# Attention transposes in two 64-row halves, with shared PSUM banks, split pools and a new written order

## The chip, the cores and the metric

One core of one Trainium2 chip. The metric is the device time of one execution in microseconds (us), the median of the runs. Engines: TensorE (PE in the rows, PEld for its weight loads), VectorE (DVE), ScalarE (ACT), GpSimd (POOL) and SyncE (SP, which here only issues DMAs).

## The reference

Three parts in a row, all in float32:

- Attention: q, k, v of shape (2, 8, 576, 64): batch 2, 8 heads, 576 positions, 64 numbers a head. q and k get a rotary embedding, then `softmax(q k^T / 8) v` for each head. The softmax divides by the sum plus 1e-9.
- A feed-forward layer on the 1152 x 512 result: `h = x @ w_in` (512 x 2048), `g = h * sigmoid(1.702 h)`, `g @ w_out`.
- A top-1 mixture of 8 experts (512 to 1024 to 512 with a ReLU) with a capacity for each expert; each token's row is scaled by the softmax probability of its expert.

## The kernel before, in words

Class `Attention` does the first part, class `Weights` loads the feed-forward weights and turns their 64-bit numbers into float32 (a "cut": three VectorE instructions, L530 to L532), class `Experts` does the rest. The change lies in `Attention` and in the constants at the top of the file.

Attention goes over 8 head pairs p (4 a batch). A pair's 576 queries are split in two halves a, each of two 128-row tiles t and 32 left over; with two heads h that makes 8 score tiles of 128 queries x 576 keys, and tile 4 holds the left-over queries of both heads. For each tile i:

- `scores` (L346, tile 4 at L337): matmuls of 64 rows (one head) against 288 keys, into a PSUM tile `s` of two banks. The two heads' matmuls stand in turn, on the upper and the lower 64 rows. TensorE does a float32 matmul in two instructions, a transpose in one.
- `least` (L358, VectorE): scales a score tile out of PSUM into `pp` and finds its minimum.
- `exps` (L370, ScalarE): exponential and row sum.
- `turn` (L389, TensorE): four 128x128 transposes of the tile into a bank `t`; `turned` (L276 on ScalarE, L277 on VectorE, both in the helper `copy`) copies the bank to `pt`.
- Columns 512 to 575 of two heads are transposed together: `rest` (L407, L409), placed in `ptr`. The reciprocals of the sums are spread over 64 columns (`spread`) and transposed (`sums`, L430, L432), placed in `tb`. `placed` copies them, with two small picks for a = 0.
- `weighted` (L451): for each half a, 10 products of v and `pt` or `ptr`, each of 128 rows x 64 columns x 288, two heads side by side, summed in PSUM bank `o`.
- `divided` (L454, VectorE): times the reciprocals; `halved` (hi at L276/L277, lo at L464): result into `xt` as a float32r number and its remainder.

PSUM of attention is 8 banks: `s` two tiles of 2, `t` three of 1, `o` 1. `next` hands out the `s` and the `t` tiles in turn. All SBUF tiles of attention come from one pool "at", all PSUM tiles from one pool "at_ps"; their room goes to `Experts` behind it.

The rotary embedding (`rope`, L321, L323) of pair 0 is on VectorE, in pieces (`START`), and of later pairs on GpSimd, two pairs ahead.

The order is written out by hand. `plan` gives every step of every pair a time: 9 units per pair, plus the tile number, plus an offset in `ORDER`; the steps are sorted by it. `pin` chains the instructions of each engine in that order, so each engine does them in this order, waiting at the head of its queue where an operand isn't ready. `ENGINES` says which engine copies what. The steps "spare" are the loads and cuts of the first 4 of 16 slices of the feed-forward weights, 8 cuts; `ORDER["spare"]` has the plan time of the first cut and the step between cuts.

Behind attention, for each weight slice, ScalarE and VectorE write a hi and a lo part (L617, L618) into a ring of 4 (`hl`, 32 KB of each partition), the first thing allocated in the room that attention had. TensorE then multiplies (`hidden`, L631, and L657) 480, 384 and 288 tokens in three passes over the slices. The first 480 tokens are all of batch 0.

Tile allocation and waits come from a scheduling layer: an instruction that writes to room which an older pool had waits for the readers of that pool.

Of the kernel before, what the change touches and what calls it, by code (L numbers as in the profile page):

```python
# [9 lines left out]
F32 = mybir.dt.float32  # L10
# [32 lines left out]
TC = {"schedule_with_timeline_sim": True}  # L43
CUT = 352
START = (
    (-7.97, 0, 0, CUT, "vector"),
    (-5.96, 1, 0, P, "vector"),
    (-5.82, 0, CUT, WIDTH, "vector"),
    (-5.66, 1, P, 2 * P, "vector"),
    (-8.85, 1, 2 * P, WIDTH, "gpsimd"),  # L50
)
# [32 lines left out]
CUTS = 0, 5, 9, 12  # L84
WIDE = max(b - a for a, b in zip(CUTS, CUTS[1:])) * TT
ORDER = {
    "scores": (-3.87, 3.28, -2.97, -0.67, -3.82, -3.5, 2.97, -3.53, -0.45),
    "least": (-2.82, -2.97, -2.63, -2.15, -2.74, -2.49, -3.28, -2.19, -2.98),
    "exps": (-2.07, -2.94, -1.17, -0.62, -2.47, -1.81, -2.57, -1.96, -2.28),
    "turn": (-0.4, -0.09, -0.77, -0.34, -0.01, -0.18, -0.84, -1.22, 0.22),  # L90
    "turned": (-0.09, 1.98, 0.73, 0.74, 0.29, 0.5, 0.71, 0.42, 0.25),
    "twice": 4.24,
    "rest": (4.75, 9.15),
    "rest_placed": (5.5, 9.76),
    "inverse": (2.9, 6.22),
    "spread": (3.76, 7.85),
    "sums": (5.5, 9.37),
    "sums_placed": (6.72, 9.92),
    "weighted": ((5.94, 5.98, 6.1, 7.03, 7.44), (9.47, 9.62, 10.57, 11.02, 11.65)),
    "divided": (8.36, 12.05),  # L100
    "halved": ((8.99, 11.5), (13.17, 15.47)),
    "rope": (-10.84, -10.42, -8.78, -9.18, -8.94, -7.53),
    "load": (-17.9, -17.6),
    "load_v": -5.18,
    "spare": (59.64, 5.42),
}


# [126 lines left out]
class Attention:  # L235


    def __init__(self, ctx, tc, qk, v, cst, xt):
        self.tc, self.nc = tc, tc.nc
        self.src = qk, v  # L240
        self.xt, self.cst = xt, cst
        self.ident = cst["ident"]
        pool = ctx.enter_context(tc.tile_pool(name="at", bufs=1))
        ps = ctx.enter_context(tc.tile_pool(name="at_ps", bufs=1, space=PSUM))
        new = self.new = lambda name, *shape: pool.tile([P, *shape], F32, name=name)
        some = lambda n, name, *shape: [new(f"{name}{i}", *shape) for i in range(n)]
        self.turns = new("turns", 2, WIDTH + 64)
        self.qk = some(3, "qk", 4, WIDTH)
        self.vr = some(2, "vr", 10, D)
        self.pp = some(4, "pp", 2, S)  # L250
        self.prem = new("prem", WIDTH)
        self.pt = new("pt", 4, 2, 2, HALF)
        self.ptr = new("ptr", 2, HALF)
        self.tb = new("tb", 2, HALF)
        self.x = some(2, "x", HALF)
        self.nm, self.sum, self.r = (some(2, name, 9) for name in ("nm", "sum", "r"))
        self.rr = some(2, "rr", 2, 2, 64)
        self.s = [ps.tile([P, 2, 512], F32, name=f"s{i}") for i in range(2)]
        self.t = [ps.tile([P, 512], F32, name=f"t{i}") for i in range(3)]
        self.o = ps.tile([P, 512], F32, name="o")[:, 0:HALF]  # L260
        self.made = {"s": 0, "t": 0}
        self.open = {}
        self.last = {}

    def next(self, of, key):
        mine = getattr(self, of)
        self.open[key] = x = mine[self.made[of] % len(mine)]
        self.made[of] += 1
        return x

    def engine(self, part):
        return getattr(self.nc, ENGINES[part])
# [56 lines left out]
    def scores(self, p, i):  # L329
# [61 lines left out]
    def turned(self, p, i):  # L391
        t = self.open.pop(("turn", p, i))
        if i == 4:
            x = t.rearrange("p (k r) -> p k r", r=32)
            out = self.pt.rearrange("p k h a c -> p (k h a) c")[:, :, 256:288]
        else:
            a, tt, h = TILES[i]
            x = t.rearrange("p (k c) -> p k c", k=4)
            out = self.pt[:, :, h, a, tt * P:(tt + 1) * P]
        self.copy(self.engine(f"t{i}"), out, x)  # L400

    def rest(self, p, a):

        t = self.next("t", ("rest", p, a))
        for tt in range(2):
            x = self.pp[2 * a + tt].rearrange("p h k -> p (h k)")[:, 512:640]
            self.nc.tensor.transpose(t[:, tt * P:(tt + 1) * P], x, self.ident)  # L407
        if a == 0:
            self.nc.tensor.transpose(t[:, 256:384], self.prem[:, 512:640], self.ident)  # L409

    def inverse(self, p, a):

# [7 lines left out]
    def spread(self, p, a):  # L420
        r = self.r[p % 2][:, 5 * a:5 * a + 4].rearrange("p (t h) -> p t h", h=2)
        self.copy(self.engine(f"rr{a}"), self.rr[a], r.unsqueeze(3).to_broadcast([P, 2, 2, 64]))

    def sums(self, p, a):

        nc = self.nc
        t = self.next("t", ("sums", p, a))
        for tt in range(2):
            x = self.rr[a][:, tt].rearrange("p h d -> p (h d)")
            nc.tensor.transpose(t[:, tt * P:(tt + 1) * P], x, self.ident)  # L430
        if a == 0:
            nc.tensor.transpose(t[:, 256:384], self.r[p % 2][:, 4:5].to_broadcast([P, P]), self.ident)  # L432

    def placed(self, p, a, kind):

        t = self.open.pop((kind, p, a))
        out = {"rest": self.ptr, "sums": self.tb}[kind]
        for h in range(2 if a == 0 else 0):
            hs = slice(h * 64, h * 64 + 64)
            x = t[hs, 256 + h * 64:320 + h * 64].rearrange("p (a r) -> p a r", a=2)  # L440
            self.copy(self.engine(f"{kind}_pick{h}"), out[hs, :, 256:288], x)
        self.copy(self.engine(f"{kind}{a}"), out[:, a, 0:256], t[:, 0:256])

    def weighted(self, p, a, n):

        v = self.vr[p % 2]
        ops = [(h, v[:, h * 4 + kt, :], self.pt[:, kt, h, a, :]) for kt in range(4) for h in range(2)]
        ops += [(h, v[:, 8 + h, :], self.ptr[:, a, :]) for h in range(2)]
        for j in range(PV[n], PV[n + 1]):
            h, x, y = ops[j]  # L450
            self.nc.tensor.matmul(self.o[h * 64:h * 64 + 64], x, y, start=j < 2, stop=j > 7)  # L451

    def divided(self, p, a):
        self.nc.vector.tensor_tensor(out=self.x[a], in0=self.o, in1=self.tb[:, a], op=ALU.mult)  # L454

    def halved(self, p, a, k):
        b, hp = divmod(p, NPAIR)
# [663 lines left out]
```

## Time and profile before

| | us |
|---|---|
| median of 3 runs | 479.53 (478.33 to 481.44) |
| the profiled execution | 481.22 |
| its span on the core | 479.5 |
| TensorE busy in the span | 452.6 (94%) |
| VectorE, ScalarE, GpSimd busy | 317.0, 263.6, 115.2 |

The profiled execution is one execution with the hardware profiler; rows are measured from the start of its span, and its own time is 1.7 us more than the span. A busy TensorE is not TensorE at its peak: a matmul's row runs from its start to a modelled end, and rows of matmuls in a queue overlap, so what a matmul costs is read from the distance of starts.

### The profile page before, as it was taken

What the parts mean: (1) busy time and instruction counts of PE and PEld (TensorE: products, weight loads), DVE (VectorE), ACT (ScalarE), POOL (GpSimd) and SP (SyncE); (2) the same over time, 40 slices, a digit from 0 to 9 for tenths busy, and PEclk for the clock granted to TensorE, in tenths of its full rate; (3) what the DMA queues carried; (4) which work ended last, traced back from release to release, by engine and by line L of the source; (5) the groups of instructions that cost most, each with busy time, mean ns of one, the idle gap of its engine ahead of it and who ended that gap; (6) DMA issues with size and microseconds to landing.
All of it is one profiled execution on the core that took longest, in us unless ns stands there. A gap on an engine that the chain in (4) does not pass through costs nothing.

```text
span 479.5 us, 8214 instructions
## 1 busy us (share of the span) xinstructions
PE 452.6 (94%) x2986; PEld 387.0 (81%) x2986; DVE 317.0 (66%) x734; ACT 263.6 (55%) x507; POOL 115.2 (24%) x100
## 2 busy tenths in 40 slices
PE   2999999999996999999999999999999999999991
PEld 1566666666664888788899999999999999999980
DVE  4667657656776898999535534457855696675661
ACT  1677877778775435244463454366566545364560
POOL 1966468448012000000000000000344023501020
PEclk9999999999999799999999999999999999999996
DMA  8514214412212485653001330002074447765510
GB/s 280 211 69 139 87 51 139 137 29 90 72 45 66 154 315 172 248 201 132 0 1 51 113 118 0 1 0 57 12 265 141 150 143 180 218 221 207 178 49 15
DMA packets 20315, 57.05 MB, mean 119 GB/s; under 512 B 3749, under 2 KB 5957, under 8 KB 20272
## 3 DMA queue, kind: packets, MB, share of 16 engines
q1 hardware_dynamic: 17584, 52.09, 32.5%
q0 software_dynamic: 1728, 3.62, 2.6%
q10 hardware_dynamic: 960, 0.79, 0.5%
q8 instruction: 25, 0.41, 0.3%
q14 instruction: 18, 0.15, 0.1%
HBM read 49.91 MB, written 6.66 MB: 118 GB/s over the span
## 4 chain that ended last, share of the span: by engine, by line
PE 69%; issue 14%; DMA 5%; DVE 5%; POOL 3%; ACT 2%; SPq 1%; POOLq 0%; DVEq 0%; ACTq 0%
PE h L631 21%; PE y L657 19%; PE s L346 8%; PE o L451 8%; PE t L389 7%; PE tr L722 2%; PE s L337 2%; POOL out L954 1%; DMA raw<-in_w_in 1%; DMA turns<-in_turns 1%; DMA slots<-entry,r_at 1%; DMA raw<-in_w_out 1%; ACT hl L617 1%; DVE pp L358 1%; POOL slots L832 1%
## 5 line engine op out<-in xcount | busy, mean ns | idle before, releaser
L631 PE MATMUL h<-xt,hl 128*128 128x288 f32 (+3 forms) x864 | 162.1, 327 | 4.7 <-ACT hl L617 4.7
L631 PEld LDWEIGHTS h<-xt,hl 128*128 128x128 f32 x864 | 137.5, 191 | 12.8 <-ACT hl L617 6.2
L657 PE MATMUL y<-gh,hl 128*128 128x288 f32 (+3 forms) x576 | 122.9, 323 | 1.5 <-ACT gh L672 0.9
L618 DVE TENSOR_TENSOR hl<-wf,hl 128x1024 fp32r<-128x1024 f32 x72 | 87.8, 1223 | 47.8 <-ACT hl L617 44.3
L617 ACT ACTIVATE hl<-wf 128x1024 fp32r<-128x1024 f32 x72 | 75.9, 1058 | 53.3 <-DVE wf L532 29.9
L657 PEld LDWEIGHTS y<-gh,hl 128*128 128x128 f32 x576 | 94.7, 188 | 5.8 <-ACT gh L667 1.2
L657 PE MATMUL y<-gl,hl 128*128 128x288 f32 (+3 forms) x288 | 75.7, 322 | 0.4 <-issue 0.4
L358 DVE TENSOR_SCALAR_CACHE_REDUCE pp<-s 128x576 f32<-128x576 f32 x64 | 46.9, 754 | 30.9 <-PE s L346 30.6
L832 POOL DMA_INDIRECT slots<-entry,r_at x12 | 13.8, 1148 | 213.6 <-DVE r_ends L746 210.5
L370 ACT ACTIVATE pp<-pp,nm 128x576 f32<-128x576 f32 x64 | 49.1, 769 | 18.4 <-DVE pp L358 18.4
L666 ACT ACTIVATE g<-h 128x480 f32<-128x480 f32 (+2 forms) x48 | 23.4, 492 | 62.8 <-PE h L631 51.4
L346 PE MATMUL s<-qk 64*128 64x288 f32 x256 | 45.6, 449 | 8.5 <-DVE qk L323 7.5
L657 PEld LDWEIGHTS y<-gl,hl 128*128 128x128 f32 x288 | 50.8, 188 | 2.9 <-issue 1.0
L321 POOL TENSOR_TENSOR qk<-qk,turns 128x640 f32<-128x640 f32 (+1 forms) x30 | 44.7, 1525 | 9.8 <-DMA qk<-in_qk 9.8
L276 ACT ACTIVATE pt<-t 128x512 f32<-128x512 f32 x64 | 37.0, 588 | 16.1 <-PE t L389 15.8
L668 DVE TENSOR_TENSOR gl<-g,gh 128x480 fp32r<-128x480 f32 (+2 forms) x48 | 26.4, 554 | 28.9 <-ACT gh L667 28.0
L346 PEld LDWEIGHTS s<-qk 64*128 64x128 f32 x256 | 25.4, 194 | 21.2 <-DVE qk L323 8.4
L389 PEld LDWEIGHTS t<-ident,pp 128*128 128x128 f32 x256 | 28.2, 142 | 14.0 <-issue 6.2
L389 PE MATMUL t<-ident,pp 128*128 128x128 f32 x256 | 38.3, 282 | 0.3 <-ACT pp L370 0.2
L451 PE MATMUL o<-pt,vr 128*64 128x288 f32 x256 | 36.5, 415 | 0.0
L464 POOL TENSOR_TENSOR xt<-x,xt 128x288 fp32r<-128x288 f32 x16 | 13.1, 820 | 63.1 <-ACT xt L276 49.2
L451 PEld LDWEIGHTS o<-pt,vr 128*64 128x64 f32 x256 | 17.0, 136 | 13.1 <-issue 5.2
(174 smaller groups left out, 481.2 us busy)
## 6 DMA issues: line engine op xcount, KB each, us to landing
wf<-in_w SPq DMA_DIRECT2D x32, 512.0 KB, 4.6
qk<-in_qk SPq DMA_DIRECT2D x14, 640.0 KB, 5.2
raw<-in_w_in SPq DMA_DIRECT2D x16, 512.0 KB, 4.5
raw<-in_w_out SPq DMA_DIRECT2D x16, 512.0 KB, 3.7
vr<-in_v SPq DMA_DIRECT2D x8, 320.0 KB, 2.9
x<-row SPq DMA_DIRECT2D x12, 192.0 KB, 2.1
out<-zero SPq DMA_DIRECT2D x9, 256.0 KB, 3.0
qk<-in_qk SPq DMA_DIRECT2D x1, 384.0 KB, 5.2
```

The costliest lines, as they stand in the source:

```text
L276: return e.activation(out=out, in_=x, func=AF.Copy)
L321: e.tensor_tensor(out=u, in0=u, in1=self.turns[:, k, ts], op=ALU.mult)
L346: nc.tensor.matmul(both[h][:, n, 0:HALF], q[hs, at:at + P], k[hs, key:key + HALF], start=True, stop=True)
L358: self.nc.vector.tensor_scalar(out=self.room(p, i).rearrange("p (n k) -> p n k", n=2), in0=self.open.pop(("s", p, i))[:, :, 0:HALF], scala ...
L370: self.nc.scalar.activation(out=x, in_=x, func=AF.Exp, scale=-1.0, bias=self.nm[p % 2][:, i:i + 1], accum_out=self.sum[p % 2][:, i:i + 1],)
L389: self.nc.tensor.transpose(t[:, cs], x[:, at:][:, cs], self.ident)
L451: self.nc.tensor.matmul(self.o[h * 64:h * 64 + 64], x, y, start=j < 2, stop=j > 7)
L617: nc.scalar.activation(out=hl[:, 0], in_=t, func=AF.Copy)
L618: self.last = nc.vector.tensor_tensor(out=hl[:, 1], in0=t, in1=hl[:, 0].bitcast(F32), op=ALU.subtract).ins
L631: self.nc.tensor.matmul(h, u, v, start=m == 0, stop=m == len(ops) - 1)
L657: nc.tensor.matmul(y[j][:, 0:w], u, v, start=f == LAG and m == 0, stop=f == n + LAG - 1 and m == 2)
L668: nc.vector.tensor_tensor(out=gl, in0=g, in1=gh.bitcast(F32), op=ALU.subtract)
```

## The change

Transposes. Every 128x128 transpose is made of two (`flip`): input rows 0 to 63 into one bank, rows 64 to 127 into another, each with a 64x64 identity, 64 columns wide. The two heads of a query tile share two banks, 512 columns each, and `turned` copies one bank (64 queries of both heads). `rest`, `sums` and tile 4 are done in the same way, and their copies take one instruction for each bank.

Banks. `t` becomes four banks, from which turns and others take two and the accumulator of `weighted` one; `take` and `leave` keep the list when the program is written.

Pools. The SBUF pool becomes three: keys (angles, q and k), turns (exponentials, sums), sums (everything else). PSUM becomes two: `s`, and the four banks.

Order and engines. All offsets in `ORDER` are new, and eleven entries of `ENGINES`. In the new order turn 1 comes before turn 0, 3 before 2, and 7, 8, 6, 5 follow each other. (A second, identical `spread` is in the text of the class; it does the same.)

```diff
 START = (
-    (-7.97, 0, 0, CUT, "vector"),
...
-    (-8.85, 1, 2 * P, WIDTH, "gpsimd"),
+    (-9.9, 0, 0, CUT, "vector"),
...
+    (-8.7, 1, 2 * P, WIDTH, "gpsimd"),
 )
 ENGINES = {
-    "t2": "vector",
-    "t3": "scalar",
+    "t2": "scalar",
+    "t3": "vector",
...
-    "twice": "vector",
-    "rr0": "scalar",
-    "rr1": "vector",
+    "twice": "scalar",
+    "rr0": "gpsimd",
+    "rr1": "scalar",
...
-    "rest_pick1": "vector",
-    "sums_pick0": "vector",
-    "sums_pick1": "vector",
-    "hix0": "vector",
-    "hix1": "scalar",
+    "rest_pick1": "scalar",
+    "sums_pick0": "scalar",
+    "sums_pick1": "scalar",
+    "hix0": "scalar",
+    "hix1": "vector",
     "lox0": "gpsimd",
-    "lox1": "gpsimd",
+    "lox1": "vector",
 }
+BANKS = 4
...
 ORDER = {
-    "scores": (-3.87, 3.28, -2.97, -0.67, -3.82, -3.5, 2.97, -3.53, -0.45),
+    "scores": (-5.69, 0, -6.18, 0, -6.33, -5.58, 0, -6.56, 0),
...
-    "turn": (-0.4, -0.09, -0.77, -0.34, -0.01, -0.18, -0.84, -1.22, 0.22),
+    "turn": (0.36, -0.78, 0.9, -0.43, -0.59, -0.22, -1.52, -3.51, -4.02),
...
-    "weighted": ((5.94, 5.98, 6.1, 7.03, 7.44), (9.47, 9.62, 10.57, 11.02, 11.65)),
+    "weighted": ((4.84, 5.34, 5.98, 7.25, 8.01), (8.68, 8.92, 10.08, 11.26, 11.41)),
...
-    "load_v": -5.18,
-    "spare": (59.64, 5.42),
+    "load_v": 0.9,
+    "spare": (58.44, 2.03),
 }
...
+        names = "at_keys", "at_turns", "at_sums"
+        keys, turns, sums = (ctx.enter_context(tc.tile_pool(name=n, bufs=1)) for n in names)
+        ps_s, ps_t = (ctx.enter_context(tc.tile_pool(name=n, bufs=1, space=PSUM)) for n in ("at_s", "at_t"))
...
+    def take(self, n, *key):
+        if key not in self.open:
+            self.open[key] = sorted(self.free[:n])
+            assert len(self.open[key]) == n
+            del self.free[:n]
+        return [self.bank[i] for i in self.open[key]]
...
+    def flip(self, banks, at, x):
+        for b in range(2):
+            bs = slice(64 * b, 64 * b + 64)
+            self.nc.tensor.transpose(banks[b][:, at:at + 64], x[bs], self.ident[bs, bs])
...
     def turn(self, p, i):
-        t = self.next("t", ("turn", p, i))
-        x = self.room(p, i)
-        at = 64 * (TILES[i] or (0, 0, 0))[2]
+        h = (TILES[i] or (0, 0, 0))[2]
+        banks = self.take(2, "turn", p, i - h)
+        x = self.room(p, i)[:, 64 * h:]
         for kt in range(4):
-            cs = slice(kt * P, (kt + 1) * P)
-            self.nc.tensor.transpose(t[:, cs], x[:, at:][:, cs], self.ident)
+            self.flip(banks, (4 * h + kt) * 64, x[:, kt * P:(kt + 1) * P])
     def turned(self, p, i):
...
         if i == 4:
+            for h, x in enumerate(self.take(2, *key)):
+                x = x[:, 0:256].rearrange("p (k a r) -> p k a r", k=4, a=2)
+                self.copy(self.engine("t4"), self.pt[:, :, h, :, 256:288], x)
+            self.leave(*key)
+            return
+        a, tt, b = TILES[i]
+        x = self.take(2, *key)[b].rearrange("p (h k c) -> p h k c", h=2, k=4)
+        at = tt * P + 64 * b
+        out = self.pt.rearrange("p k h a c -> p h k a c")[:, :, :, a, at:at + 64]
         self.copy(self.engine(f"t{i}"), out, x)
+        self.leave(*key, only=b)
```

## Rows read from the trace of the kernel before

**Rows 1.** The page, busy time of each engine and its share of the span

```profile
PE 452.6 (94%) x2986; PEld 387.0 (81%) x2986; DVE 317.0 (66%) x734; ACT 263.6 (55%) x507; POOL 115.2 (24%) x100
```

**Rows 2.** Windows: length; busy PE, PEld, DVE, ACT, POOL; clock; DMA share; GB/s

```profile
60.45:77.42 16.97, 16.97 (x124) 11.24 (x126) 11.06 (x34) 12.81 (x31) 10.71 (x9) 1.00 0.30 98
150.82:154.52 3.70, 0.26 (x3) 0.01 (x1) 3.24 (x11) 1.56 (x3) 1.68 (x2) 1.00 0.00 0
154.52:162.00 7.48, 6.97 (x18) 5.36 (x19) 7.12 (x10) 3.57 (x4) 0.00 (x0) 0.54 0.57 190
```

**Rows 3.** Timeline of PE in that pair: start, duration, instructions, idle time before

```profile
59.85 0.60 PE L389 MATMUL t<-ident,pp 128*128 128x128 f32 x4
...
62.95 1.24 PE L346 MATMUL s<-qk 64*128 64x288 f32 x8
64.12 1.09 PE L389 MATMUL t<-ident,pp 128*128 128x128 f32 x8
65.05 0.38 PE L407 MATMUL t<-ident,pp 128*128 128x128 f32 x2
65.27 1.14 PE L337 MATMUL s<-qk 128*128 128x288 f32 x4
66.24 0.38 PE L430 MATMUL t<-ident,rr 128*128 128x128 f32 x2
66.56 1.19 PE L451 MATMUL o<-pt,vr 128*64 128x288 f32 x8
67.68 1.09 PE L389 MATMUL t<-ident,pp 128*128 128x128 f32 x8
```

**Rows 4.** Timeline of PE behind attention

```profile
150.29 0.79 PE L451 MATMUL o<-ptr,vr 128*64 128x288 f32 x3
154.52 0.96 PE L631 MATMUL h<-xt,hl 128*128 128x480 f32 x2 [3.44 <-ACT hl L617]
155.98 8.04 PE L631 MATMUL h<-xt,hl 128*128 128x480 f32 x24 [0.51 <-ACT hl L617]
...
165.59 2.33 PE L631 MATMUL h<-xt,hl 128*128 128x480 f32 x10
```

**Rows 5.** Timeline of ACT behind attention

```profile
153.41 1.06 ACT L617 ACTIVATE hl<-wf 128x1024 fp32r<-128x1024 f32 x1 [1.26 <-POOL xt L464]
```

**Rows 6.** Weight loads: timeline of two short windows, then their groups (mean ns)

```profile
62.95 0.19 PEld L346 LDWEIGHTS s<-qk 64*128 64x128 f32 x2 [0.44 <-issue]
...
64.12 0.20 PEld L389 LDWEIGHTS t<-ident,pp 128*128 128x128 f32 x2 [0.39 <-issue]
...
L346 PEld LDWEIGHTS s<-qk 64*128 64x128 f32 x256 | 25.4, 194 | 21.2 <-DVE qk L323 8.4
L389 PEld LDWEIGHTS t<-ident,pp 128*128 128x128 f32 x256 | 28.2, 142 | 14.0 <-issue 6.2
```

**Rows 7.** Timeline of PE later: transposes with 96 moving columns

```profile
371.15 0.49 PE L927 MATMUL tg<-ident,got 96*128 96x96 f32 x4
```

**Rows 8.** ACT's groups in the pair: copies out of PSUM (busy us, mean ns)

```profile
L276 ACT ACTIVATE pt<-t 128x512 f32<-128x512 f32 x8 | 4.6, 588 | 1.9 <-PE t L389 1.9
...
L276 ACT ACTIVATE tb<-t 128x256 f32<-128x256 f32 x2 | 0.8, 390 | 0.8 <-DVE tb L277 0.8
```

**Rows 9.** Timeline of ACT, two exponentials with a read-out between them

```profile
78.45 0.77 ACT L370 ACTIVATE pp<-pp,nm 128x576 f32<-128x576 f32 x1
...
79.20 0.76 ACT L370 ACTIVATE pp<-pp,nm 128x576 f32<-128x576 f32 x1
```

**Rows 10.** DVE's groups from 140 to 205: the weight cuts (busy us, mean ns)

```profile
L531 DVE SCALAR_TENSOR_TENSOR m<-raw,m 128x512 uint32<-128x512 uint32 x21 | 14.3, 688 | 0.3
L532 DVE SCALAR_TENSOR_TENSOR wf<-raw,m 128x512 uint32<-128x512 uint32 x19 | 13.5, 714 | 0.4
...
L530 DVE TENSOR_SCALAR m<-raw 128x512 uint32<-128x512 uint32 x21 | 8.7, 421 | 1.4 <-DMA raw<-in_w_in 0.8 <-DMA raw<-in_w_out 0.6
```

**Rows 11.** Waits of PE from 150 to 245: us, times, longest

```profile
PE h L631 <- ACT hl L617: 4.7, 3, 3.4
```

More of the change, by code (lines that the diff above doesn't have):

```diff
@@ L242, in __init__ @@
         self.ident = cst["ident"]
[L243 to L260, printed above, removed]
@@ L261, in __init__, with some @@
-        self.made = {"s": 0, "t": 0}
-        self.open = {}
+        names = "at_keys", "at_turns", "at_sums"
+        keys, turns, sums = (ctx.enter_context(tc.tile_pool(name=n, bufs=1)) for n in names)
+        ps_s, ps_t = (ctx.enter_context(tc.tile_pool(name=n, bufs=1, space=PSUM)) for n in ("at_s", "at_t"))
+        def some(pool, n, name, *shape):
+            return [pool.tile([P, *shape], F32, name=f"{name}{i}") for i in range(n)]
+        self.turns, = some(keys, 1, "turns", 2, WIDTH + 64)
@@ new lines, in __init__ @@
+        self.qk = some(keys, 3, "qk", 4, WIDTH)
+        self.warm, = some(keys, 1, "warm", 2)
+        self.pp = some(turns, 4, "pp", 2, S)
+        self.prem, = some(turns, 1, "prem", WIDTH)
+        self.nm, self.sum, self.r = (some(turns, 2, name, 9) for name in ("nm", "sum", "r"))
+        self.pt, = some(sums, 1, "pt", 4, 2, 2, HALF)
+        self.ptr, = some(sums, 1, "ptr", 2, HALF)
+        self.tb, = some(sums, 1, "tb", 2, HALF)
+        self.vr = some(sums, 2, "vr", 10, D)
+        self.x = some(sums, 2, "x", HALF)
@@ L263, in __init__, with score_room @@
+        self.rr = some(sums, 2, "rr", 2, 2, 64)
+        self.s = [ps_s.tile([P, 2, 512], F32, name=f"s{i}") for i in range(2)]
+        self.bank = [ps_t.tile([P, 512], F32, name=f"t{i}") for i in range(BANKS)]
+        self.free = list(range(BANKS))
+        self.made = 0
+        self.open, self.left = {}, {}
         self.last = {}
[L265 to L268, printed above, removed]
-        return x
+    def score_room(self, p, i):
+        self.open["s", p, i] = x = self.s[self.made % len(self.s)]
+        self.made += 1
+        return x
@@ new lines, in take, with leave @@
+    def take(self, n, *key):
[4 more added lines that the diff above has]
+        return [self.bank[i] for i in self.open[key]]
+    def leave(self, *key, only=None):
+        for n, i in enumerate(self.open[key]):
+            if only in (None, n):
+                self.free.append(i)
+        self.left[key] = self.left.get(key, 0) + 1
+        if only is None or self.left[key] == 2:
+            del self.open[key]
@@ L339, in scores @@
         a, t, _ = TILES[i]
-        both = [self.next("s", ("s", p, i + h)) for h in range(2)]
+        both = [self.score_room(p, i + h) for h in range(2)]
         for n in range(2):
@@ L408, in rest @@
         if a == 0:
-            self.nc.tensor.transpose(t[:, 256:384], self.prem[:, 512:640], self.ident)
+            self.flip(banks, 128, self.prem[:, 512:640])
     def inverse(self, p, a):
@@ L422, in spread @@
         self.copy(self.engine(f"rr{a}"), self.rr[a], r.unsqueeze(3).to_broadcast([P, 2, 2, 64]))
+    def spread(self, p, a):
+        r = self.r[p % 2][:, 5 * a:5 * a + 4].rearrange("p (t h) -> p t h", h=2)
+        self.copy(self.engine(f"rr{a}"), self.rr[a], r.unsqueeze(3).to_broadcast([P, 2, 2, 64]))
     def sums(self, p, a):
[L426 to L427 removed]
+        banks = self.take(2, "sums", p, a)
         for tt in range(2):
[L429 to L430 removed]
+            self.flip(banks, tt * 64, self.rr[a][:, tt].rearrange("p h d -> p (h d)"))
         if a == 0:
[L432 removed]
+            self.flip(banks, 128, self.r[p % 2][:, 4:5].to_broadcast([P, P]))
     def placed(self, p, a, kind):
[L436 removed]
+        banks = self.take(2, kind, p, a)
         out = {"rest": self.ptr, "sums": self.tb}[kind]
@@ L439, in placed @@
             hs = slice(h * 64, h * 64 + 64)
-            x = t[hs, 256 + h * 64:320 + h * 64].rearrange("p (a r) -> p a r", a=2)
+            x = banks[h][hs, 128:192].rearrange("p (a r) -> p a r", a=2)
             self.copy(self.engine(f"{kind}_pick{h}"), out[hs, :, 256:288], x)
-        self.copy(self.engine(f"{kind}{a}"), out[:, a, 0:256], t[:, 0:256])
+        for b, x in enumerate(banks):
+            x = x[:, 0:128].rearrange("p (t c) -> p t c", t=2)
+            self.copy(self.engine(f"{kind}{a}"), out[:, a, 0:256].rearrange("p (t b c) -> p b t c", t=2, b=2)[:, b], x)
+        self.leave(kind, p, a)
     def weighted(self, p, a, n):
         v = self.vr[p % 2]
+        o = self.take(1, "o", p, a)[0][:, 0:HALF]
         ops = [(h, v[:, h * 4 + kt, :], self.pt[:, kt, h, a, :]) for kt in range(4) for h in range(2)]
@@ L450, in weighted @@
             h, x, y = ops[j]
-            self.nc.tensor.matmul(self.o[h * 64:h * 64 + 64], x, y, start=j < 2, stop=j > 7)
+            self.nc.tensor.matmul(o[h * 64:h * 64 + 64], x, y, start=j < 2, stop=j > 7)
     def divided(self, p, a):
-        self.nc.vector.tensor_tensor(out=self.x[a], in0=self.o, in1=self.tb[:, a], op=ALU.mult)
+        o = self.take(1, "o", p, a)[0][:, 0:HALF]
+        self.nc.vector.tensor_tensor(out=self.x[a], in0=o, in1=self.tb[:, a], op=ALU.mult)
+        self.leave("o", p, a)
     def halved(self, p, a, k):
```

51 lines of the change are left out of this document (22 added, 29 removed).

## The prediction

> **What bounds the kernel now.** I read the engine shares of the page first, then the windows, then the TensorE timeline of one head pair. The page says that TensorE (PE) is busy 94% of the span and no other engine over 66% [rows 1]. That alone doesn't say what the attention stage is worth, so I took one steady pair of heads, 60.45 to 77.42 us: PE is busy all 16.97 us of it, ScalarE (ACT) 12.81, VectorE (DVE) 11.06, GpSimd (POOL) 10.71 [rows 2]. So eight pairs are paced by PE, some 136 us, and whatever takes PE time out of a pair takes it out of the end.
>
> The timeline shows what a pair of PE is made of [rows 3]. Four transposes in a row take 0.60 us, the last one 0.27, so they start (0.60 - 0.27) / 3 = 0.109 us apart. Eight score matmuls start at 62.95 and the next work at 64.12: 1.17 us. Eight weighted matmuls: 66.56 to 67.68, 1.12. Four scores of tile 4: 65.27 to 66.24, 0.97. Around them sits a cost that no instruction owns: PE pays when the shape of the used array changes (64x128 for scores, 128x128 for transposes and tile 4, 128x64 for weighted). The two transposes at 66.24 take 0.22, but the weighted matmuls behind them start after 0.32. Where the shape stays there is nothing: from 64.12 ten transposes (1.09) lead to tile 4's scores at 65.27 (0.06 of 1.15 is the entry), and those lead to transposes in 0.97 = 4 x 0.242, which is also what two score matmuls side by side take. So of eight scores 4 x 0.242 = 0.97 is work and 0.20 the change; of eight weighted 0.96 is work and 0.16 the change.
>
> Sum of one pair: scores 4 x 0.97 = 3.87, tile 4 0.97, weighted 40 matmuls in 20 steps 20 x 0.241 = 4.82, transposes (36 + 5 + 5) x 0.109 = 5.01: 14.67. The remaining 2.30 of 16.97 are the 12 changes of shape that the written order has in a pair, 0.19 each.
>
> The second cost is behind the last pair. PE ends it at 151.08 and starts the first expert matmul of the feed-forward at 154.52 after 3.44 us of waiting for ACT's ring copy; two matmuls later it waits 0.51 more and runs from 155.98 [rows 4]. ACT's ring copy itself waited for POOL's last xt [rows 5]: the ring lies in the memory of the attention pool, which is given back whole. In these 3.70 us PE is busy 0.26; then, to 162, its granted clock is 0.54, so most of that at the lower level (1.2 GHz), where 24 matmuls take 8.04 us against (2.33 - 0.38) / 9 = 0.217 each later, 5.2 for 24 [rows 2, 4].
>
> **The change part by part.**
>
> *Transposes.* Each 128x128 transpose becomes two with 64 rows and 64 moving columns, one in the upper and one in the lower half of the array, into different banks. Do halves run side by side? The scores are such halves: two loads of 64x128, of 194 ns each, lie together within 0.19 us [rows 6], and 0.242 us for two matmuls of 288 columns says the same of the streams. What would such a step cost? The time follows the moving columns: 96 columns take (0.49 - 0.25) / 3 = 0.081 [rows 7], 128 take 0.109, so 64 give 0.055. The load must keep up: two loads of 128 columns, 142 ns each, lie within 0.20 us, so they start 60 ns apart [rows 6]. I take 0.060 for the two halves; 46 x 0.060 = 2.76, 2.25 less than now. Bounds: 0.055 (2.53) below; above, no gain (0.109), and 2 x 0.109 if halves don't overlap at all.
>
> A rule speaks against it. The Trainium skill, "TensorE: Matmul & The Clock Gate", section "LDWEIGHTS (loading the stationary operand)", says that a load costs its columns over 1.2 GHz whatever its rows. By it a half still pays 107 ns and the step stays at 0.107 us, so the transposes would gain nothing. The trace disagrees for transposes: loads of 128 columns start 60 ns apart and are not what spaces 96-column transposes at 81 ns [rows 6, 7]; no row shows it for 64 rows.
>
> *Changes of shape.* Scores and transposes now share 64x128. Following the new order through one pair (turn, turn, scores, sums, three weighted, two turns, rest, scores, five turns, scores, three weighted, tile 4, two weighted, rest, scores, sums, two weighted) gives 8 changes where there were 12: 1.53 us, 0.77 less. PE then has 9.66 + 2.76 + 1.53 = 13.96 us a pair.
>
> *Copies.* Each bank now holds half of two tiles, so a copy has the same 512 columns as before. Tile 4, rest and sums copy two banks instead of one: a 256-column copy is 0.39 us and a 512-column one 0.59 [rows 8], so by the line through the two, 128 columns cost 0.29 and 64 columns 0.24 (estimates), and two half copies 0.19 more than one; four on ACT, 0.8. By the engine table ACT also takes the repeated tail and three picks (4 x 0.24 = 0.96), and swaps one hi copy, one spread and one turned copy for another. ACT's 12.81 becomes 14.5 by summed busy time. Back to back its instructions overlap by some 0.1 us each (one exponential is listed with 0.77, yet the next one, with a read-out between them, starts 0.75 after it [rows 9]), so a saturated ACT needs about 13.2. ACT is therefore next, at 13.2 to 14.5, level with PE. DVE loses the tail, a spread, three picks and gains one lo part and one split copy: about 10.5 of 11.06. POOL trades a lo part (0.8) for a spread: 10.7 or less, still below.
>
> *Waits between them.* Turns, rests, sums and the weighted accumulator draw on four banks in all. The tightest place by the order is five turns in a row: the fifth pair of banks waits for ACT's two tile-4 copies, which stand behind an exponential; PE may wait 0.4 us there, and the score matmuls queued behind it with it. With two engines level I take 14.65 a pair, 0.15 above ACT's upper number; from 13.96 to 15.5. Eight pairs: 8 x (16.97 - 14.65) = 18.6 us off.
>
> *Weight cuts.* They start at 58.44 in the plan and now come every 2.03 units instead of 5.42 (a unit is a ninth of a pair, 1.63 us). A cut is three DVE instructions, 0.42 + 0.69 + 0.71 = 1.82 us [rows 10]. From 58.44 to the last score tile at 65.5 DVE has 11.5 us; its own work is 7.06 x 10.5 / 9 = 8.2 and four cuts add 7.3: 4 over. Score reductions queue behind the cuts, and PE behind those. I take 3 us lost, 0 to 4. The other four cuts stand before DVE's last divisions, which PE doesn't need for the first tokens.
>
> *Pools.* The ring (32 KB a partition) now lies inside the pool of keys, free after the last scores, and the score banks are apart. The ring copies can run during the last pair's turns. Of the 4.9 us from 151.08 to 155.98 I take 4 off (0 to 4.9); of the 2.8 us that the low clock costs, 2 (0 to 2.8), since without an idle stretch it has no reason to fall. Later waits of PE on ring copies (4.7 in all, 4.0 of them counted already [rows 11]) give 1 with more cuts done early (0 to 1.1).
>
> Loads of V later in the queue, ropes in another order and the first pair's start order cost nothing by my reading: the loads of a pair are issued in the pair before, POOL has 4 us of slack a pair, and the start on DVE keeps its order. If that cover is gone, a late rope would show once a pair as a wait of PE on POOL, and the 0.85 us between 14.65 and the upper end of 15.5 is what I leave for it.
>
> **Sum**, against the profiled execution's 481.22: -18.6 + 3 - 4 - 2 - 1 = -22.6, so 458.6. The median of the runs shown is 1.7 lower than that execution: 457.
>
> **Rivals.**
> 1. *The load binds the halves*, or halves follow one another at 0.060 (0.109 to 0.120 a step). PE: 9.66 + 5.0 to 5.5 + 1.53 = 16.2 to 16.7, so 2 to 6 off in eight pairs, and the end part about -6: 467 to 472. For it: no row has a 64-row transpose, and the rule above. Against: [rows 6, 7]. Chance 0.18.
> 2. *The halves don't overlap and the short form of the load is lost*: each half at 0.109, a step of 0.218. PE 10.0 + 9.66 + 1.53 = 21.2 a pair, 34 more in all, the end part -6: 507. It is slower from the step at which 8 x (9.66 + 46x + 1.53 + 0.7 - 16.97) + 3 - 7 = 0, x = 0.121 us. For it: twice the instructions. Against: scores do overlap. Chance 0.10.
> 3. *The new pools free nothing*, because the expert work is still put behind the last attention instruction: the end part is +3 instead of -4, so 464. Within the likeliest case's range.
> 4. *ACT is a wall at 16 to 17 a pair* through waits on banks, and hides most of the gain: 472 to 479. Chance 0.04.
>
> **How the numbers follow.** The forecast has 0.68; its own range is 446 (13.96 a pair, all of the end) to 466. Faster by over 1% takes the forecast, rival 1 and its neighbours, 0.86; within 1%, which is about what a measurement of this kernel can't tell from no change, 0.04; slower 0.10. The range for 8 in 10 goes from 445 to 473 and takes in rival 1.
>
> **What would show it.** Pairs every 14 to 15 us in the timeline, transposes in twos some 60 ns apart, two starting within 10 ns; 8 shape changes of 0.19; ACT over 13 us busy in a pair; no PE gap over 1 us between the last weighted and the first expert matmul, with the clock at 1.00. Steps of 109 ns or more would make rival 1 or 2 right; a pair of 14 us with a long gap after it, rival 3.

## The result, and the profile after

The changed kernel takes 465.14 us (median of 4 runs, 465.04 to 465.18), the kernel before 479.22 beside it (4 runs): a ratio of 0.970, interval 0.967 to 0.973. A second measurement on another chip gave 0.968 (0.965 to 0.971). The forecast was 457, with a range of 445 to 473.

The page of the kernel after, busy time of each engine and its share of the span (463.4 us), then its group of transposes, which answers to [rows 1]:

```profile
PE 434.7 (94%) x3354; PEld 375.0 (81%) x3354; DVE 306.2 (66%) x710; ACT 271.9 (59%) x571; POOL 117.7 (25%) x100
...
L405 PE MATMUL t<-ident,pp 64*128 64x64 f32 x576 | 31.3, 231 | 1.1 <-DVE x L488 0.6
```

The shares are what they were, but for ScalarE's (55% before). The difference is inside the stages. Windows of the kernel after: one steady pair, the end of attention, the rest of the first pass of the feed-forward, and the stretch from VectorE's first weight cut to its last (columns as in [rows 2]):

```profile
73.40:88.10 14.70, 14.70 (x169) 9.85 (x168) 9.52 (x30) 13.79 (x40) 10.39 (x9) 1.00 0.31 110
116.00:151.50 35.50, 30.94 (x269) 20.09 (x267) 30.22 (x63) 25.52 (x64) 5.18 (x5) 1.00 0.34 114
151.50:233.00 81.50, 80.26 (x372) 69.23 (x373) 67.80 (x117) 35.54 (x52) 0.00 (x0) 1.00 0.46 157
116.60:215.60 99.00, 93.20 (x549) 73.20 (x545) 89.60 (x170) 50.77 (x99) 5.18 (x5) 1.00 0.50 170
```

Timeline of PE after, one steady pair and then the end of attention (`t<-pt,vr` are the weighted matmuls, `h<-xt,hl` and `y<-gh,hl` the feed-forward); it answers to [rows 3, 4]:

```profile
73.36 1.68 PE L484 MATMUL t<-pt,vr 128*64 128x288 f32 x12
...
79.84 0.71 PE L405 MATMUL t<-ident,pp 64*128 64x64 f32 x16
80.39 1.19 PE L365 MATMUL s<-qk 64*128 64x288 f32 x8
81.42 0.28 PE L405 MATMUL t<-ident,rr 64*128 64x64 f32 x4
...
85.38 1.78 PE L405 MATMUL t<-ident,pp 64*128 64x64 f32 x32
86.94 1.24 PE L365 MATMUL s<-qk 64*128 64x288 f32 x8
88.12 1.19 PE L484 MATMUL t<-pt,vr 128*64 128x288 f32 x8
...
131.35 0.77 PE L405 MATMUL t<-ident,pp 64*128 64x64 f32 x17
132.05 4.61 PE L666 MATMUL h<-xt,hl 128*128 128x480 f32 x20
...
146.41 0.66 PE L484 MATMUL t<-ptr,vr 128*64 128x288 f32 x4
147.00 2.87 PE L666 MATMUL h<-xt,hl 128*128 128x480 f32 x12
151.48 0.67 PE L692 MATMUL y<-gh,hl 128*128 128x480 f32 x2 [1.61 <-DVE x L488]
```

What to see. Sixteen half transposes (79.84) are followed by scores after 0.55 us. Of that the first step of two halves, behind a change of shape, takes 0.11; the seven behind it take the other 0.44, 0.062 each, where whole transposes took 0.109. The pair takes 14.76 (88.12 - 73.36) instead of 16.97, and ACT is busy 13.79 of it. At the end of attention the gap of [rows 4] is gone: feed-forward matmuls start at 147.00, right behind the last weighted ones, 24 of them even stand among the last pair's steps (20 in the row at 132.05), and the granted clock stays at 1.00. What is left of the wait, 1.61, stands at 151.48 and is for the last division. From 116 us on VectorE is busy 30.22 of 35.5, then 67.80 of 81.5; TensorE is busy 80.26 of the same 81.5.

For the account I cut both spans at the same four places: the first weighted matmul of pair 0, that of pair 6, the last weighted matmul, and the last `y` matmul of the second pass (384 tokens).

| us | before | after | difference |
|---|---|---|---|
| start to pair 0 | 26.4 | 28.7 | +2.3 |
| six pairs | 101.8 | 89.2 | -12.6 |
| pair 6 to last weighted | 22.4 | 28.7 | +6.3 |
| to the end of the second pass | 167.4 | 156.8 | -10.6 |
| the rest | 161.4 | 159.9 | -1.5 |

The third and fourth lines belong together, since 24 feed-forward matmuls (5.2 us at 0.217) moved from the one into the other: -4.3 in all. The sum is -16.1 in the profiled executions, and -14.1 in the medians.

### The profile page after: what moved, and what is told of

It is laid out like the page before. It is cut to its first block, busy times and chain, and to the rows that moved or that the text cites. A ratio compares the mean times of both kernels' runs of the same rounds, so it can differ in the third digit from the quotient of the medians.

```text
span 463.4 us, 8915 instructions
## 1 busy us (share of the span) xinstructions
PE 434.7 (94%) x3354; PEld 375.0 (81%) x3354; DVE 306.2 (66%) x710; ACT 271.9 (59%) x571; POOL 117.7 (25%) x100
## 4 chain that ended last, share of the span: by engine, by line
PE 57%; issue 14%; DVE 10%; DMA 8%; POOL 4%; ACT 4%; SPq 0%; POOLq 0%; DVEq 0%; ACTq 0%
PE h L666 18%; PE y L692 16%; PE s L365 6%; PE t L484 6%; PE t L405 5%; DMA slots<-entry,r_at 2%; DMA raw<-in_w_out 2%; POOL slots L867 2%; PE s L356 2%; DVE pp L377 2%; PE tr L757 2%; POOL out L989 2%; DVE m L566 2%; DMA ent<-slots 2%; DVE wf L567 1%
## 5 line engine op out<-in xcount | busy, mean ns | idle before, releaser
L666 PE MATMUL h<-xt,hl 128*128 128x288 f32 (+3 forms) x864 | 159.4, 323 | 1.5 <-DVE r L442 0.6
L666 PEld LDWEIGHTS h<-xt,hl 128*128 128x128 f32 x864 | 135.4, 188 | 9.0 <-ACT hl L652 2.0
L653 DVE TENSOR_TENSOR hl<-wf,hl 128x1024 fp32r<-128x1024 f32 x72 | 88.1, 1226 | 50.3 <-ACT hl L652 50.1
L867 POOL DMA_INDIRECT slots<-entry,r_at x12 | 15.1, 1258 | 202.7 <-DVE r_m L781 178.7
L365 PEld LDWEIGHTS s<-qk 64*128 64x128 f32 x256 | 27.2, 199 | 16.2 <-DVE qk L342 8.8
L295 ACT ACTIVATE pt<-t 128x512 f32<-128x512 f32 (+1 forms) x72 | 36.1, 553 | 4.0 <-PE t L405 3.0
L484 PE MATMUL t<-pt,vr 128*64 128x288 f32 x256 | 37.9, 418 | 0.0
L405 PEld LDWEIGHTS t<-ident,pp 64*128 64x128 f32 x576 | 24.5, 138 | 14.1 <-ACT tb L295 3.1
L405 PE MATMUL t<-ident,pp 64*128 64x64 f32 x576 | 31.3, 231 | 1.1 <-DVE x L488 0.6
L484 PEld LDWEIGHTS t<-pt,vr 128*64 128x64 f32 x256 | 15.6, 136 | 13.1 <-issue 3.1
L702 ACT ACTIVATE gh<-g 128x480 fp32r<-128x480 f32 (+2 forms) x48 | 25.0, 526 | 1.1
```

Source lines behind the costliest of these rows:

```text
L295: return e.activation(out=out, in_=x, func=AF.Copy)
L365: nc.tensor.matmul(both[h][:, n, 0:HALF], q[hs, at:at + P], k[hs, key:key + HALF], start=True, stop=True)
L405: self.nc.tensor.transpose(banks[b][:, at:at + 64], x[bs], self.ident[bs, bs])
L484: self.nc.tensor.matmul(o[h * 64:h * 64 + 64], x, y, start=j < 2, stop=j > 7)
L653: self.last = nc.vector.tensor_tensor(out=hl[:, 1], in0=t, in1=hl[:, 0].bitcast(F32), op=ALU.subtract).ins
L666: self.nc.tensor.matmul(h, u, v, start=m == 0, stop=m == len(ops) - 1)
```

## Experiments

Each is a version of the changed kernel, unless it is called "the kernel before with". Ratios are to the kernel before, on the same chip.

**Whole transposes in the new order.** The same order, engines, pools and number of copies, with 128x128 transposes into one bank of the two. Shown is `turn` alone; `rest`, `sums` and the copies are changed to match.

```diff
-            self.flip(banks, (4 * h + kt) * 64, x[:, kt * P:(kt + 1) * P])
+            cs = slice(kt * P, (kt + 1) * P)
+            self.nc.tensor.transpose(banks[h][:, cs], x[:, cs], self.ident)
```

> The changed kernel with whole 128x128 transposes in place of the two halves (one bank of the two is used; order, engines, number of copies, pools as changed). Theory (halves side by side are the gain): 46 transposes at 0.109 in place of 0.057 us are 2.4 us a pair, and the order then has 15 changes of shape in a pair in place of 8, 7 x 0.19 = 1.3 more: a pair of 18.4 us in place of 14.76, 25 to 29 us more in all, 490 to 494. Rival (ScalarE is the wall at 14.8 a pair and the transposes only fill its shadow): under 3 us more, 465 to 468.

480.17 us, 0.997 (0.994 to 1.000). Timeline of PE in this kernel, the starts of two pairs:

```profile
63.97 1.68 PE L486 MATMUL t<-pt,vr 128*64 128x288 f32 x12
...
81.20 1.19 PE L486 MATMUL t<-pt,vr 128*64 128x288 f32 x8
```

That lies between the two expectations: 17.23 us a pair. Against 14.76 the halves are worth 2.5 a pair, and in the whole 0.997 - 0.970 = 0.027, 13 us. The steps alone make 46 x (0.109 - 0.062) = 2.2 of the 2.5. The rest is little, although this order has 15 changes of shape with whole transposes and 8 with halves: the halves' pair loses time elsewhere (a stall on banks, below). With whole transposes all the rest of the change together is worth some 1.5 us, 0 to 3 by the interval. Halves in the kernel before, in its own order, were not run.

**Halves issued one group after the other**: the four upper halves of a turn, then the four lower ones.

```diff
-        for kt in range(4):
-            self.flip(banks, (4 * h + kt) * 64, x[:, kt * P:(kt + 1) * P])
+        for b in range(2):
+            bs = slice(64 * b, 64 * b + 64)
+            for kt in range(4):
+                at = (4 * h + kt) * 64
+                self.nc.tensor.transpose(banks[b][:, at:at + 64], x[bs, kt * P:(kt + 1) * P], self.ident[bs, bs])
```

> The changed kernel with the turns issued as four upper halves and then four lower halves, not in turn. Theory (halves overlap only because neighbours use different rows of the array): the eight steps of a tile take 7 x 0.055 = 0.39 us in place of 0.23, 1.4 us a pair, 16.2 in place of 14.76, and 10 to 12 us in all. Rival (TensorE is not what a pair waits for, or it overlaps them anyhow): a pair of 14.8 to 15.1.

465.25 us, one run. Timeline of PE in this kernel, a run of 16 halves:

```profile
80.78 0.76 PE L416 MATMUL t<-ident,pp 64*128 64x64 f32 x16
81.33 1.24 PE L365 MATMUL s<-qk 64*128 64x288 f32 x8
```

Again 0.55 us: the theory falls. Eight steps' time for 16 halves doesn't need an upper and a lower half as neighbours; at a distance of four instructions the order in which they are issued doesn't matter.

**Cuts at the old spacing.**

```diff
-    "spare": (58.44, 2.03),
+    "spare": (59.64, 5.42),
```

> The changed kernel with the weight cuts at the old plan times (first 59.64, step 5.42). Theory (eight cuts in 23 us are more than VectorE's slack and cost TensorE about 3 us at the end of attention): 2 to 4 us less at the last weighted matmul, of which the feed-forward takes 1 to 2 back: 462 to 464. Rival (the cuts hide in waits that are there anyway and their early end pays for the feed-forward): 466 to 469.

472.92 us, 0.983 (0.980 to 0.986): 6 us worse than the change, more than either side expected. The last weighted matmul is 4.2 earlier (142.5), as the theory has it, but the second pass ends 9.4 later (312.8). The profiled execution, at 476.84, is 3.9 above the median, so of the 9.4 only a part stands for the others. Window of the first pass from its first `y` matmul in this kernel, then two rows of its PE timeline:

```profile
144.50:242.20 97.70, 90.92 (x395) 76.02 (x396) 79.57 (x135) 39.34 (x56) 0.46 (x1) 0.95 0.44 153
149.62 3.56 PE L666 MATMUL h<-xt,hl 128*128 128x480 f32 x10 [0.85 <-DVE hl L653]
154.78 1.17 PE L666 MATMUL h<-xt,hl 128*128 128x480 f32 x2 [1.60 <-ACT hl L652]
```

TensorE now waits in the pass: some 6.7 us idle, most of it for ring copies, whose weights are cut later. Behind the first of these waits its granted clock is at the lower level, 1.2 GHz, from 150.6 to 160.8 us, hence the mean of 0.95.

**Cuts a little wider.**

```diff
-    "spare": (58.44, 2.03),
+    "spare": (58.44, 2.6),
```

> The changed kernel with the weight cuts every 2.6 plan units instead of 2.03; the last one, at 76.6, still stands before the end of the written order. Theory (from the first cut to the end of the 480-token pass VectorE is the engine that counts, and a cut moved within that stretch only moves its 1.8 us; only cuts that leave attention lengthen the pass): the last weighted matmul starts 1 to 3 us earlier, the 480-token pass is as much longer, and the whole is 0.996 to 1.006 of the changed kernel, 0.966 to 0.976 of the kernel before. Rival (the cuts pressed together are what costs some 10 us at the end of attention): 2 to 4 us below the changed kernel, 0.961 to 0.965 of the kernel before, with no longer pass behind it.

465.54 us, 0.969 (0.967 to 0.972): the theory's number. The first `y` comes 1.8 earlier (149.6). Counted from pair 0's first weighted matmul, which is 0.9 later in this profile, the last weighted one is 1.0 earlier and the end of the second pass 0.4.

**Cuts early**, from plan time 30 on, every 4.5 units, and **cuts in chosen places**: one a pair in pairs 3 to 6, each 4.5 units into its pair, then one at 62.5 and one every 2 units behind it (`plan` takes the list in place of a first time and a step).

```diff
-    "spare": (58.44, 2.03),
+    "spare": (30.0, 4.5),
```

> The changed kernel with the first cut at 30.0 and a step of 4.5 units, so that two cuts fall in each pair, where VectorE has about 4 us to spare. Theory (the crowding of the cuts costs about 3 us): 461 to 462.5, pairs stay within 14.7 to 15.0. Rival (the loss at the end of attention is the chain of the last pair itself, not the cuts): 464.5 to 466.

480.70 us, 0.998 (0.996 to 1.000): all of the gain is lost, which neither side expected.

```diff
-    "spare": (58.44, 2.03),
+    "spare": (31.5, 40.5, 49.5, 58.5, 62.5, 64.53, 66.56, 68.6),
```

> The changed kernel with the weight cuts at 31.5, 40.5, 49.5, 58.5, 62.5, 64.53, 66.56 and 68.6: three of them a pair apart behind VectorE's second reciprocal, where VectorE waits about 1 us for scores and GpSimd waits 3 us for ScalarE. Theory (a cut early costs what it delays in VectorE's queue: the earlier try put cuts ahead of a copy that frees a bank and beside GpSimd's ropes): 0.5 to 1 us for each of three pairs, 2 to 4 us back at the end, so 1 to 2 us less than the changed kernel. Rival (any cut in a steady pair costs TensorE its full 1.8 us or more): 2 to 5 us more.

468.97 us, 0.975 (0.972 to 0.978): some 3 us worse, as the rival had it. Pairs take up to 20.6 us in the first of these, and 0.6 to 1.8 more in the second. Timeline of VectorE, GpSimd and PE at such a cut in the first:

```profile
87.30 1.62 DVE L565 TENSOR_SCALAR m<-raw 128x512 uint32<-128x512 uint32 x1
88.95 0.69 DVE L566 SCALAR_TENSOR_TENSOR m<-raw,m 128x512 uint32<-128x512 uint32 x1
89.68 0.69 DVE L567 SCALAR_TENSOR_TENSOR wf<-raw,m 128x512 uint32<-128x512 uint32 x1
90.29 0.68 DVE L296 COPY pt<-t 128x512 f32<-128x512 f32 x1
...
87.10 1.53 POOL L340 TENSOR_TENSOR qk<-qk,turns 128x640 f32<-128x640 f32 x1
...
91.03 0.46 PE L405 MATMUL t<-ident,prem 64*128 64x64 f32 x7 [2.55 <-DVE pt L296]
```

The cut stands in front of the copy that empties a bank, TensorE waits 2.55 us for that copy, and beside a rope instruction the cut's first instruction takes 1.62 instead of 0.42 [rows 10]. In none of the places tried did a pair in front of the last two have room for a cut.

**Three picks back on VectorE.**

```diff
-    "rest_pick1": "scalar",
-    "sums_pick0": "scalar",
-    "sums_pick1": "scalar",
+    "rest_pick1": "vector",
+    "sums_pick0": "vector",
+    "sums_pick1": "vector",
```

> The changed kernel with three picks (the second of rest, both of sums) on VectorE as before. Theory (ScalarE is level with TensorE and makes TensorE wait some 0.8 us a pair for banks and exponentials): 0.5 to 0.7 us less on ScalarE, a pair of 14.3 to 14.6, ratio to the changed kernel 0.992 to 0.997. Rival (TensorE alone sets the pair): 14.76 and a ratio of 0.998 to 1.002, or worse if VectorE's queue delays the division.

476.77 us, 0.991 (0.988 to 0.994): worse than the numbers of both sides; only the rival's "or worse" allowed for it. Timelines of PE and DVE in this kernel, a pair:

```profile
62.50 1.68 PE L484 MATMUL t<-pt,vr 128*64 128x288 f32 x12
...
70.86 1.24 PE L365 MATMUL s<-qk 64*128 64x288 f32 x8 [1.16 <-DVE pp L377]
...
78.92 1.43 PE L484 MATMUL t<-pt,vr 128*64 128x288 f32 x10
...
68.04 0.47 DVE L296 COPY tb<-t 64x64 f32<-64x64 f32 x2 [1.89 <-PE t L405]
```

16.42 a pair: though VectorE is busy under 10 of 14.7 us in the change, three small copies in its queue cost 1.7. Two of them make it wait 1.89 us for TensorE's transposes of the sums, with the next score tiles' `least` behind them in its order; TensorE then waits 1.16 for `least` (70.86). In a pair so dense it isn't the sum of an engine that counts but what stands ahead of its next urgent instruction.

**One pool of each kind.**

```diff
-        keys, turns, sums = (ctx.enter_context(tc.tile_pool(name=n, bufs=1)) for n in names)
-        ps_s, ps_t = (ctx.enter_context(tc.tile_pool(name=n, bufs=1, space=PSUM)) for n in ("at_s", "at_t"))
+        keys = turns = sums = ctx.enter_context(tc.tile_pool(name="at", bufs=1))
+        ps_s = ps_t = ctx.enter_context(tc.tile_pool(name="at_ps", bufs=1, space=PSUM))
```

> The changed kernel with one SBUF pool and one PSUM pool for attention. Theory (split pools close the stretch behind attention and keep the clock up): ring copies wait again for the last xt, TensorE idles 4 to 5 us behind the last weighted matmul, its granted clock falls for some 7 us, and the time is 4 to 7 us longer: 469 to 472. Rival (the matmuls put between the last pair's transposes delay attention by as much as they save): 464 to 466.

468.99 us, 0.975 (0.972 to 0.978). Timeline of PE in this kernel behind attention:

```profile
142.16 0.66 PE L483 MATMUL t<-ptr,vr 128*64 128x288 f32 x4
146.09 0.70 PE L665 MATMUL h<-xt,hl 128*128 128x480 f32 x2 [3.28 <-ACT hl L651]
147.04 9.20 PE L665 MATMUL h<-xt,hl 128*128 128x480 f32 x34 [0.25 <-ACT hl L651]
```

The gap of [rows 4] is back, with a wait of 3.28 on the same ring copy. But the last weighted matmul is 4.3 earlier than with split pools (142.4), since nothing is put among the last pair's steps. So the pools are worth 2.5 to 3.4 us (by the two measurements of the change, 0.970 and 0.968), not the whole gap.

**One pool of PSUM, split SBUF.**

```diff
-        ps_s, ps_t = (ctx.enter_context(tc.tile_pool(name=n, bufs=1, space=PSUM)) for n in ("at_s", "at_t"))
+        ps_s = ps_t = ctx.enter_context(tc.tile_pool(name="at_ps", bufs=1, space=PSUM))
```

> The changed kernel with one PSUM pool, and the three SBUF pools as they are. Theory (the split of PSUM lets the first expert matmuls in between the last pair's transposes, where they take banks and TensorE from a pair that is still waiting; the split of SBUF is what removes the ring's wait): the last weighted matmul starts near 142.4 as with one pool each, no wait of over 1 us on the ring copy behind it, expert matmuls from about 143.5, 463 to 467 us, 0.994 to 1.002 of the changed kernel. Rival (the split of PSUM is what pays): as with one pool of each kind, about 2.5 us above the changed kernel, with a wait on the ring copy or on the last division.

466.42 us, 0.974 (0.971 to 0.978). No feed-forward matmul stands among the last pair's steps, and they start at 146.8, after 1.8 us of waiting for the last division. The ratio, 0.4% above the change's, speaks for the rival, but the intervals overlap, and in its profile the second pass ends when it does in the change (303.4). Which of the two splits pays is left open.

**The kernel before with the new spacing of the cuts.**

```diff
-    "spare": (59.64, 5.42),
+    "spare": (58.44, 2.03),
```

> The kernel before with one part of the change alone: the first weight cut at 58.44 and the next ones every 2.03 units. Theory (in the kernel before, attention is paced by TensorE at 16.97 a pair and VectorE has room, so cuts beside the last pairs cost little, and they fall out of the feed-forward pass): -2 to +1 us against the kernel before. Rival (as in the changed kernel, the cuts hold back the last pair's VectorE steps): the last weighted matmul 4 to 6 us later, and +1 to +4 us in all.

483.72 us, 1.009 (1.006 to 1.011), 4.2 us slower: the rival's direction, and its upper end.

**The kernel before with split pools.** The lines of the pools as in the change's diff.

> The kernel before with one part of the change alone: three SBUF pools and two PSUM pools (scores, and the other four banks). Theory (the prediction's: the ring's copies run beside the last pair's turns): the 4.9 us between the last weighted matmul and steady expert matmuls go, and the low clock behind them, -3 to -8 us against the kernel before. Rival (as in the changed kernel: expert matmuls are put among the last pair's steps and wait there): the last weighted matmul 2 to 6 us later, and -3 to 0 us in all.

483.02 us, 1.007 (1.004 to 1.010). Neither theory nor rival had a loss. Timelines of PE at the end of attention, first of the kernel with the cuts, then of the one with the pools:

```profile
154.95 0.66 PE L451 MATMUL o<-ptr,vr 128*64 128x288 f32 x4
158.69 2.12 PE L631 MATMUL h<-xt,hl 128*128 128x480 f32 x4 [3.09 <-ACT hl L617]
```

```profile
143.81 0.67 PE L635 MATMUL h<-xt,hl 128*128 128x480 f32 x2 [0.27 <-DVE pp L362]
...
145.66 2.43 PE L635 MATMUL h<-xt,hl 128*128 128x480 f32 x10 [0.41 <-DVE hl L622]
...
156.51 0.67 PE L661 MATMUL y<-gh,hl 128*128 128x480 f32 x2 [1.43 <-DVE x L458]
...
161.06 2.43 PE L635 MATMUL h<-xt,hl 128*128 128x480 f32 x10 [0.55 <-DVE hl L622]
```

With the cuts alone the ring still can't be written before attention ends, so their early weights wait. With the pools alone the ring's room is there, but the weights aren't: TensorE idles 1.4 us instead of 4.0 between the last weighted matmul and the first `y`, and 6.2 instead of 1.1 in the rest of the first pass.

**What ties these together** looks at first like the moment when VectorE ends its last weight cut. Here it is in the timelines of DVE, before and after:

```profile
228.79 0.68 DVE L532 SCALAR_TENSOR_TENSOR wf<-raw,m 128x512 uint32<-128x512 uint32 x1
```

```profile
214.90 0.69 DVE L567 SCALAR_TENSOR_TENSOR wf<-raw,m 128x512 uint32<-128x512 uint32 x1
```

| us | first cut | last cut ends | VectorE idle between | end of second pass | behind the last cut | TensorE idle in the first pass |
|---|---|---|---|---|---|---|
| before | 126.4 | 229.5 | 12.4 | 318.1 | 88.6 | 1.1 |
| after | 116.6 | 215.6 | 9.4 | 303.4 | 87.9 | 1.2 |
| whole transposes | 130.8 | 227.2 | 7.2 | 315.6 | 88.5 | 1.5 |
| cuts at the old spacing | 119.3 | 224.4 | 17.0 | 312.8 | 88.4 | 6.7 |
| cuts a little wider | 117.5 | 215.7 | 8.9 | 303.9 | 88.1 | 2.4 |
| before, split pools | 127.4 | 232.1 | 14.7 | 320.6 | 88.5 | 6.2 |
| one PSUM pool | 117.4 | 213.9 | 8.4 | 303.4 | 89.5 | 0.0 |
| one pool of each kind | 117.3 | 209.8 | 5.5 | 304.9 | 95.1 | 0.0 |
| before, new cuts | 124.6 | 223.8 | 6.7 | 319.3 | 95.5 | 0.0 |

(VectorE's idle time is the window from first to last cut less its busy time in it; after, 99.00 - 89.60. TensorE's is counted from the first `y` matmul to the last one with 480 tokens.) In the first seven kernels the second pass ends 87.9 to 89.5 us behind the last cut, wherever that lies between 214 and 232 us, and in the five profiles that the table leaves out it is 87.5 to 88.3. But a fixed distance doesn't tell which engine waits for the other. Over 70 us of it is the second pass itself, in which TensorE has no idle time in any profile.

What tells is TensorE's own idle time in the first pass. In the change it is 1.2 of 81.8 us, so there TensorE itself sets the end, and earlier cuts could give back no more than that behind the first `y`. No run leaves the cuts out to show it more directly. VectorE only just keeps up: it idles 5.0 of the 68.5 us from the last weighted matmul to its last cut. With the cuts at the old spacing and split pools, in either order (lines 4 and 6), TensorE idles over 6 us, and there the cuts do hold it up. The kernel before has that wait in front of the pass, in its gap: 4.0 us idle there and 1.1 in the pass. What differs is how many cuts are done when attention ends: 3 of 32 at the old spacing, and the last cut ends 77 to 82 us behind the last weighted matmul; 6 to 8 in all the others, and it ends 65 to 69 us behind it. An early first cut alone doesn't help: in the kernels with cuts early and in chosen places it stands at 69.7 and 73.4, but the last one ends at 228.5 and 218.7, since attention itself is longer.

In the last three, with dense cuts, TensorE doesn't idle in the pass at all; in the last two of them it has lost the time before, at the ring. So spacing and pools are one edit in two parts: each without the other leaves the other's limit standing. That they gain when put together in the kernel before, with its own order, was not run.

## Why the prediction was right, and where its numbers failed

*The halves: right.* 0.062 us a step behind the first, and 0.060 was forecast. A rule of the Trainium skill ("TensorE: Matmul & The Clock Gate", "LDWEIGHTS (loading the stationary operand)") gives a load the time of its 128 columns over 1.2 GHz, and by it a step would have stayed at 0.107 (an estimate); that made rival 1. The traces don't agree: only the first step of a run of halves, behind a change of shape, takes 0.11. Rival 2, halves that don't overlap, fell with the same row.

*The pair: right, a little short.* Forecast 14.65; four of the six pairs take 14.76 or 14.77, two 15.05 and 15.10, the average is 14.87: 2.10 off a pair instead of 2.32. TensorE is busy all of it. To the 9.66 of matmuls that I had add 46 x 0.062 = 2.85 for the halves and 0.6 for the stall on banks in five turns in a row (85.38, 16 steps in 1.56; forecast 0.4). What is left, 1.65, are the changes of shape, 1.53 in the forecast, together with the crossings between scores and transposes, which share 64x128 and yet cost some 0.06 (81.42 - 80.39 = 1.03 for 0.97 of work), where I had put nothing. That 14.65 came so close is in part luck: I had put it just above ScalarE's upper number, 14.5, and ScalarE is busy 13.79 of 14.70.

*The first pair: the largest miss, 4.6 us.* Of eight pairs I took 2.32 off each, and I costed the first one's new order at nothing. But what stands before pair 0's first weighted matmul grew by 2.3 instead of shrinking. The next pair's scores now come earlier in the order, so one more block of them stands there (27.34 to 28.73 us), and before it TensorE waits 1.05 and 0.80 us for VectorE's `least` and a copy. In all profiles of the new order pair 0 starts its weighted matmuls at 28.1 to 30.5, of the old at 26.4 to 27.4. No run puts the old start into the new order, so the cause is read from the timeline alone.

*The end: right in kind, too large in size.* TensorE does pace it, as I read from its 94%. From pair 6 to the last weighted matmul a pair's gain, 2.3, and 3 lost to the cuts make 0.7 more by my forecast. It is 23.5 (28.7 less 5.2 of feed-forward work) where it was 22.4, so 1.1 more. With the cuts at the old spacing the same stretch takes 23.9 with 12 feed-forward matmuls (2.6), so 21.3: the dense cuts cost some 2.2 there, within my 0 to 4. Behind it I expected 7 us off (gap 4, clock 2, later ring waits 1) and found 5.4: TensorE's idle time fell from 4.0 to 1.6 (2.4 off), the low clock went (2.8 off), and the later waits stayed (1.1 and 1.2). What I left out of the price of the cuts is their use: undone, they cost 6 us, because TensorE then waits in the first pass.

*The pools.* I took 6 for gap and clock; putting the single pools back costs 2.5 to 3.4 us. Rival 3, where the pools free nothing, is not what happened, but its time (464) was the nearest, for another reason: the first pair.

*The sum.* In us, between the same places as in the first table:

| | forecast | found |
|---|---|---|
| start to pair 0 | -2.3 | +2.3 |
| six pairs | -13.9 | -12.6 |
| pair 6 to last weighted, less 5.2 | +0.7 | +1.1 |
| to the end of the second pass, with the 5.2 | -7.0 | -5.4 |
| the rest | 0 | -1.5 |
| together | -22.6 | -16.1 |

Of the 1.5 gained in the last stage I can't say what it is; single profiles of that stage differ by more (159 to 165 us). The other 1.7 of the 8.1 between 457 and 465.1 is the step from the profiled execution to the median: the one before lay above its median, the one after on it.

## What to carry to other kernels

When two engines are nearly full, neither the larger busy share nor a fixed distance between one engine's step and the end tells which of them sets the end: engines in step keep that distance whoever waits. Look at the idle time of each in the stretch, and at whom it waits for (here 1.2 of 81.8 us in the change, 6.7 of 98.0 with the cuts at the old spacing). A gap closed on the busy engine gives time back only if its next operands are ready. Two edits that free the same resource from two sides, room in the ring and data for it, should be costed together: alone, each of them made the kernel before slower by 0.7 to 0.9%.

## What the hardware showed beside that

Sixteen halves take 0.55 us whether upper and lower ones alternate or come four and four. The rows don't name the half that an instruction uses, so whether TensorE starts lower halves ahead of upper ones written before them stays open.

The first instruction of VectorE's cut, which reads and writes SBUF alone, takes 1.62 us instead of 0.42 beside a rope instruction of GpSimd, and it ended 0.3 us behind that instruction (88.92 and 88.63). The same shows in the change beside an `xt` instruction of GpSimd: 0.99 us, and an end 0.29 behind (140.82 and 140.53). The Trainium skill ("SBUF — State Buffer", "SBUF: two separate sides") says that the two engines share a pair of ports, which is held for a whole instruction by the one that starts first, if VectorE's instruction runs in a mode that uses the pair or has two inputs in SBUF. The ends agree with that; whether this instruction runs in such a mode no row shows, and no run here separates the ports from other causes.
